# Mirrored Fourier columns, k transposed by transfers from pair 7 on, and pair 7's loads between the two weight matrices

## The chip, the cores and the metric

The kernel runs on one core of a Trainium2 chip. The metric is the device time of one execution in microseconds (us). The engines are named as in the profile: PE (TensorE, matrix products), DVE (VectorE), ACT (ScalarE), POOL (GpSimd), and SP (SyncE, which here only issues DMAs). PE writes to PSUM, which has eight banks of 512 f32 columns; POOL does not touch PSUM in this kernel.

## What is computed

A block-sparse attention (4 batches, 8 heads, 768 rows, 64 columns a head; each row sees its own block of 64 keys and up to three more that its gate scores pick, causally), and on its output a Fourier mix with a two-layer network:

```python
k_rep = k.reshape(B, H, n_blocks, block, D).mean(axis=3)
gate_scores = np.einsum('bhsd,bhnd->bhsn', q, k_rep)
gate_scores = np.where(causal, gate_scores, -1000000000.0)
top_idx = np.argsort(gate_scores, axis=-1)[..., -top_k:]
...
scores = np.where(mask & (pos[:, None] >= pos[None, :]), scale * q @ k.T, -1000000000.0)
x = softmax(scores) @ v
...
X = np.fft.fft(x, axis=1)
X = np.fft.fft(X, axis=2)
u = x + np.real(X)
un = (u - mu) / np.sqrt(var + 1e-06)
out = u + np.maximum(un @ w_ch1, 0.0) @ w_ch2
```

## The kernel before

All operations are first written down as a list (`Plan.op`: rank, engines with a cost in us, what is read and written). A planner (`Plan.schedule`, `Plan.search`) then places them on the engines by these costs, in simulated time, and after some hundred random changes of ranks and release times emits the program in the order found. So the order on each engine is fixed when the program is built, by the costs in the list; a change of a cost, of an operation or of the seed gives another order everywhere. `LANDING`, `LAT` and `SLACK` are what the planner adds for transfers, semaphores and PE's inputs; `rel` is the earliest time of an operation; `FILL_TO` says until when PE's waits are filled with matmuls on a tile of zeros (`warm`, `filler`, L476), which keep its clock up.

**Attention** (`attention(p)`) works on 16 pairs of heads, four pairs to a batch. A pair's q, k, v are loaded by SP (L453). POOL, ACT or DVE casts them to f16; q also gets the remainder of the cast, so that 128 rows (64 of the cast, 64 of the remainder) stand for a head in `qhl`. For pairs 0 to 6 PE transposes q (`q_turn`, L620) into PSUM, and DVE or ACT copies it to `QG`; from pair 7 on SP issues transposing transfers instead (L611). k's cast of all pairs is transposed by PE (`k_turn`, L564) and copied by ACT or DVE (L780, L781) to rows 0 to 63 of `KI`, whose rows 64 to 75 hold an indicator of the 12 key blocks. The block sums of k give the gate scores of q (L583, L600, L635, L640), DVE picks the best three of them (L674 and on), and the choice, turned by PE (L699), is written as 0 or -60000 into rows 64 to 75 of `QG` (L709). So the score product over 76 rows (L732) adds the mask by itself. ACT takes the exponential (L743), POOL cuts the diagonal blocks (L749), PE multiplies with v (L761), and DVE divides into `x` (L770, L773).

**Fourier** (`fourier(b)`) comes once all four pairs of a batch are there. It folds x by symmetry (L793, L804, L814), takes the first step over the rows on PE (`stage1`, L832, L836) with a copy to `ty` and a mirrored one to `tr`, and the second step over the columns for each of six row tiles (`stage2`, L866): two matmuls of 256 columns for the even and two for the odd output columns. DVE adds x (L872) and takes the statistics (L879, L882); the normed rows are transposed to `unT`, for batch 0's first half by PE (L930), otherwise by transfers of SP (L922).

**The network** (`mlp(b)`): `up` (L1034) with the ReLU on ACT or DVE (L1046, L1048), `down` (L1063) with the add to u (L1069) and the store. For the last batch `down` is done with seven products of quarter matrices instead of eight (`down_seven`, L1008, sums at L957 and L1014). The products of one batch lie between the attention of the next ones. POOL issues the loads of the two weight matrices (L457), with a cast on the way, w1 from 37 us and w2 from 51.4 us on in the planner's time.

`Plan.schedule` models POOL's and SP's transfers as sharing the bandwidth by half.

## Time and profile before

| | us |
|---|---|
| median of 3 runs | 295.85 (295.43 to 295.97) |
| the profiled execution | 295.36 |
| its span | 293.6 |
| PE busy | 287.7 |
| DVE busy | 210.5 |
| ACT busy | 185.0 |
| POOL busy | 129.2 |

The span runs from the first to the last instruction; 1.8 us lie around it. Busy time is the time in which an engine had at least one instruction in work; matmuls overlap one another, and fillers count as busy. In a group's row stand the line, engine, operation, out<-in, shapes and count, then the busy us and the mean ns of one, then the idle time just before them and what ended it.

### The profile page before, as it was taken

The numbers are of one execution on the slowest core, as the hardware profiler recorded it, in microseconds if no ns is written. First come the engines' busy times: TensorE is split into PE (matmuls) and PEld (weight loads), VectorE is DVE, ScalarE is ACT, GpSimd is POOL, SyncE is SP. The second block draws the span as 40 slices with busy tenths as digits, with TensorE's granted clock in tenths as the row PEclk, the third lists the DMA queues.
The fourth block names the chain that finished last, engine by engine and source line by source line (L and its number), as shares of the span: only waits on it lengthen the run. The fifth ranks groups of instructions, "written<-read, shape, count | busy, mean of one in ns | idle before, by whom it ended". The sixth has DMA issues, their size and how long they took to land.

```text
span 293.6 us, 8001 instructions
## 1 busy us (share of the span) xinstructions
PE 287.7 (98%) x3002; PEld 194.6 (66%) x3002; DVE 210.5 (72%) x704; ACT 185.0 (63%) x407; POOL 129.2 (44%) x251
## 2 busy tenths in 40 slices
PE   8999999999999999999999999999999999999995
PEld 4677777766656677567656776656766554566884
DVE  4899999995454869876458899589588801057884
ACT  3589998969718687478757747819941760577000
POOL 5568986765849618666731595823200000000000
PEclk9999999999999999999999999999999999999999
DMA  8999999999588951788596157470000403100132
GB/s 211 250 237 210 221 241 219 212 208 218 112 207 196 167 113 29 119 197 125 54 250 169 39 135 153 90 127 36 3 18 20 116 20 96 57 2 0 38 108 71
DMA packets 108773, 37.41 MB, mean 127 GB/s; under 512 B 101192, under 2 KB 104948, under 8 KB 108736
## 3 DMA queue, kind: packets, MB, share of 16 engines
q1 hardware_dynamic: 104272, 32.06, 50.4%
q0 software_dynamic: 3536, 4.56, 8.6%
q8 instruction: 23, 0.38, 0.6%
q10 hardware_dynamic: 928, 0.30, 0.4%
q14 instruction: 14, 0.11, 0.1%
HBM read 28.52 MB, written 6.29 MB: 119 GB/s over the span
## 4 chain that ended last, share of the span: by engine, by line
PE 89%; DVE 5%; ACT 2%; DMA 2%; issue 1%; POOL 0%; DVEq 0%; POOLq 0%
PE bank L1034 26%; PE bank L1063 21%; PE bank L732 12%; PE bank L761 7%; PE bank L1008 6%; PE bank L866 4%; PE bank L476 3%; DMA loads<-in_q_dram 2%; PE bank L564 1%; PE bank L620 1%; PE bank L832 1%; PE bank L583 1%; ACT ty L780 1%; PE bank L727 1%; DVE tr L781 1%
## 5 line engine op out<-in xcount | busy, mean ns | idle before, releaser
L743 ACT ACTIVATE turned<-bank 128x512 f16<-128x512 f32 (+1 forms) x192 | 89.7, 601 | 12.5 <-PE bank L732 12.1
L1034 PE MATMUL bank<-unT,w 128*128 128x384 f16 x512 | 90.7, 326 | 0.0
L1046 ACT ACTIVATE hT<-bank 128x384 f16<-128x384 f32 x114 | 56.7, 501 | 37.5 <-PE bank L1034 36.8
L1034 PEld LDWEIGHTS <-w 128*128 128x128 f16 x512 | 48.4, 98 | 29.7
L1063 PE MATMUL bank<-w,hT 128*128 128x512 f16 x288 | 67.9, 379 | 0.0
L732 PE MATMUL bank<-turned,keys 76*128 76x128 f16 (+3 forms) x384 | 51.2, 258 | 0.3 <-DVE tr L781 0.2
L1063 PEld LDWEIGHTS <-hT 128*128 128x128 f16 x288 | 26.6, 97 | 26.5
L749 POOL TENSOR_SCALAR_AFFINE_SELECT turned<-turned 128x512 f16<-128x512 f16 (+1 forms) x44 | 22.4, 529 | 38.8 <-ACT turned L743 28.0
L732 PEld LDWEIGHTS <-keys 76*128 76x128 f16 x384 | 29.8, 97 | 12.8 <-issue 0.5
L761 PEld LDWEIGHTS <-turned 128*128 128x128 f16 x672 | 23.7, 97 | 4.2 <-ACT turned L743 0.6
L1069 DVE TENSOR_TENSOR u<-bank,u 128x512 f32<-128x512 f32 x18 | 12.4, 689 | 19.3 <-PE bank L1063 19.1
L761 PE MATMUL bank<-vals,turned 128*128 128x65 f16 x672 | 25.1, 193 | 0.0
L552 POOL TENSOR_TENSOR loads<-loads 128x384 f16<-128x384 f32 x25 | 22.9, 915 | 4.1 <-DVE fs L793 3.1
L709 DVE TENSOR_SCALAR turned<-bank 12x384 f16<-12x384 f16 x64 | 20.6, 321 | 3.2 <-PE bank L699 1.4
L547 POOL TENSOR_TENSOR turned<-loads,turned 128x320 f16<-128x320 f32 x25 | 19.8, 792 | 1.4 <-DVE fs L793 0.8
L773 DVE TENSOR_TENSOR x<-bank,rcp 128x384 f16<-128x384 f32 x32 | 17.6, 553 | 0.8
L780 ACT COPY keys<-bank 64x768 f16<-64x768 f16 x14 | 11.1, 794 | 11.1 <-PE bank L564 8.6
L476 PE MATMUL bank<-warm 128*128 128x512 f16 x58 | 16.3, 412 | 1.3 <-DVE warm L464 1.3
L781 POOL CAST loads<-loads 128x384 f16<-128x384 f32 x24 | 12.3, 514 | 11.4 <-issue 3.0
L872 DVE TENSOR_TENSOR u<-bank,x 128x512 f32<-128x512 f32 x24 | 15.2, 670 | 0.9 <-PE bank L866 0.9
L879 DVE BATCH_NORM_STATS2 bst<-u 128x6 f32<-128x512 f32 x24 | 15.7, 671 | 0.0
L1014 DVE TENSOR_TENSOR u<-u,bank 128x256 f32<-128x256 f32 x36 | 13.1, 415 | 3.1 <-PE bank L1008 2.2
(110 smaller groups left out, 403.1 us busy)
## 6 DMA issues: line engine op xcount, KB each, us to landing
loads<-in_k_dram SPq DMA_DIRECT2D x28, 192.0 KB, 3.4
loads<-in_v_dram SPq DMA_DIRECT2D x28, 192.0 KB, 3.7
loads<-in_q_dram SPq DMA_DIRECT2D x26, 192.0 KB, 3.5
out_dram<-u SPq DMA_DIRECT2D x18, 256.0 KB, 2.3
w<-in_moe_w_ch_dram POOLq DMA_DIRECT2D x16, 256.0 KB, 6.9
out_dram<-u SPq DMA_DIRECT2D x12, 128.0 KB, 1.7
hT<-in_k_dram SPq DMA_DIRECT2D x4, 192.0 KB, 4.5
hT<-in_q_dram SPq DMA_DIRECT2D x4, 192.0 KB, 3.9
```

Of the source, the lines that this page charges most:

```text
L476: nc.tensor.matmul(bank32[P.SPARE], warm[:, 0:128], warm, start=True, stop=True)
L547: lambda x, n, hi=hi, lo=lo, e=e: eng[x].tensor_tensor(out=lo, in0=qn[a][:, e, 1:NST], in1=hi[:, 1:NST], op=OP.subtract),
L552: lambda x, n, kh=kh, kl=kl, e=e: eng[x].tensor_tensor(out=kl, in0=kn[a][:, :, e, :], in1=kh, op=OP.subtract),
L709: nc.vector.tensor_scalar(out=rows[:, i::2, :], in0=turned[at:at + NB, 0:3 - i, :], scalar1=-NEG, scalar2=NEG, op0=OP.mult, op1=OP.add)
L732: nc.tensor.matmul(bank32[sp.bank][:, co:co + a1 - a0], KI[e][g3][0:76, 128 * jt:128 * jt + 128], QG[e][g3][0:76, a0:a1], start=not added, ...
L743: lambda x, n, sp=sp, pt=pt, at=at, wid=wid: nc.scalar.activation(out=pt[:, at:at + wid], in_=bank32[sp.bank][:, 0:wid], func=AF.Exp, scal ...
L749: lambda x, n, pt=pt, at=at, nd=nd: nc.gpsimd.affine_select(out=pt[:, at:at + 128 * nd].rearrange("p (a c) -> p a c", a=nd), in_=pt[:, at: ...
L761: nc.tensor.matmul(o[:, st, 0:65], pt[:, col:col + 128], V16[v4][:, e, jt, 0:65], start=(i == 0), stop=(i == 20))
L1008: nc.tensor.matmul(bank32[mp.bank][:, 0:256], A[i][:, z, :], Bm[i][:, z, :], start=(z == 0), stop=(z == 7))
L1034: nc.tensor.matmul(bank32[hp_.bank][:, 0:384], w1[:, dt, 128 * it:128 * it + 128], unT[:, dt, 384 * hf:384 * hf + 384], start=(dt == 0), s ...
L1046: nc.scalar.activation(out=o, in_=i_, func=AF.Relu)
L1063: nc.tensor.matmul(bank32[cp.bank], hT[hf][:, it, 128 * j:128 * j + 128], w2[:, it, :], start=(it == 0), stop=(it == NIT - 1))
```

## The change

- Second Fourier step of batches 1 to 3 (`SYM`): the cosine part is even and the sine part odd in the column number, so the new `stage2_half` computes columns 0 to 255 of each part's half only (256, 129, 128 and 128 columns in four matmuls), laid out plainly in one bank. The mirrored columns come from it by sums: a copy of 256 columns out of PSUM (`bsb`), two adds of x of 256 columns out of PSUM, and two sums of 255 columns in SBUF on DVE or POOL. A 256-column table joins the constants.
- k of pairs 7 to 15 (`TURN_K`): k's cast goes into `kx`, 256 columns a row tile: indicator, k of head 0, k of head 1, indicator. SP's transposing transfers bring it to `KI` in two pieces a pair, and PE's transposes and the copies are left out. The two heads now have their rows in opposite order (`AT`), and head 0's scores run over 128 rows (`ROWS`) whose unused ones are zero in `KI`; `kx` and `KI` are prepared by memsets, and the indicator comes by four transfers instead of one.
- Loads: pair 7's wait for w1's last piece, w2 is issued from 55 us on, and loads may be released from 50 instead of 60 us.
- The planner shares bandwidth by `SHARE`, and searches 700 rounds with seed 8 (600 with seed 7 before).
- Memory: small tiles are cut from one, fewer buffers for `rcp` and `bst`, `lnv` joined with `nmr`, `warm` put on `bsb`. In `stage1` the extra matmuls on `xm` come earlier in the group.

```diff
...
@@ -89,6 +93,7 @@
     DEPTH = 5
+    SHARE = dict(POOL=1.5, SP=3.0)
@@ -290,7 +295,8 @@
                 shared = max(0.0, dma_free[other] - go)
-                dma_free[mine] = go + (2 * o.dma if 2 * o.dma <= shared else o.dma + shared / 2)
+                f = self.SHARE[mine]
+                dma_free[mine] = go + min(f * o.dma, o.dma + shared * (1.0 - 1.0 / f))
@@ -320,6 +326,9 @@
 LATE = 2600
+SYM = (1, 2, 3)
+W2 = 55.0
+TURN_K = 7
...
@@ -489,16 +510,30 @@
 
+    for i in range(NH):
+        small(3000, {"DVE": 0.5, "POOL": 0.9}, 0,
+              lambda x, n, i=i: [eng[x].memset(kx[i][:, :, at:at + 64], 0.0) for at in (0, 192)][-1],
+              w=[("kone", i)])
+
+        def ones(x, n, i=i):
+            flat = kx[i].rearrange("p s c -> p (s c)")
+            for lo in range(2):
+                for at in (lo, 192 + lo):
+                    r = eng[x].memset(flat[64 * lo:64 * lo + 64, at:at + 5 * 258 + 1:258], 1.0)
+            return r
+        small(3000, {"DVE": 0.24, "POOL": 0.62}, 0, ones, r=[("kone", i)], w=[("kone", i)])
+
...
 
-    def load(p, rank, what, e, q_="SP"):
+    def load(p, rank, what, e, q_="SP", r=()):
...
         dma(rank, q_, dst, src[b, 2 * hp + e].rearrange("(st p) d -> p st d", p=128),
-            [(t, i, e)], 0.72 if p < 3 else 0.85, rel=0.0 if p < 7 else max(60.0, release(p) - 18.0))
+            [(t, i, e)], 0.72 if p < 3 else 0.85, r=r,
+            rel=0.0 if p < 7 else max(50.0, release(p) - 18.0))
@@ -511,8 +546,12 @@
     const(0.6, "POOL", own24, dr["own24"].ap().rearrange("p (a c) -> p a c", a=5), ["own24"], 0.3, 3.3)
-    const(0.7, "POOL", ki_all[64:64 + NB], dr["IndR"].ap().unsqueeze(1)
-          .to_broadcast([NB, 2 * NG, S]), [("kind", e, i) for e in range(2) for i in range(NG)], 0.3, 4.0)
+    small(0.3, "DVE", 0.45, lambda x, n: nc.vector.memset(ki_all[0:64, :, :, 0, :], 0.0), w=["kz"])
+    for e in range(2):
+        for i in range(NG):
+            dma(0.7, "POOL", KI[e][i][64 - AT[e]:64 - AT[e] + NB],
+                dr["IndR"].ap().rearrange("n (s c) -> n s c", s=NST),
+                [("kind", e, i)], 0.1, r=["kz"] if e == 0 else [], rel=4.0)
@@ -530,13 +569,15 @@
             for e in range(2):
-                load(p, at_, "k", e)
-                load(p, at_, "q", e)
+                load(p, at_, "k", e, r=[("w1", 3, 1)] if p == HP + 3 else ())
+                load(p, at_, "q", e, r=[("w1", 3, 1)] if p == HP + 3 else ())
             for e in range(2):
-                load(p, at_ + (0.1 if p < 3 else 500), "v", e)
+                load(p, at_ + (0.1 if p < 3 else 500), "v", e,
+                     r=[("w1", 3, 1)] if p == HP + 3 else ())
         for e in range(2):
-            hi, lo = qhl[h2][:, e, :, 0:64], qhl[h2][:, e, 1:NST, 64:128]
-            kh, kl = k16[h2][:, :, 64 * e:64 * e + 64], klo[0][:, :, 64 * e:64 * e + 64]
+            hi = qhl[h2][:, e, :, AT[e]:AT[e] + 64]
+            lo = qhl[h2][:, e, 1:NST, 64 - AT[e]:128 - AT[e]]
+            kh, kl = kx[h2][:, :, 64 + 64 * e:128 + 64 * e], klo[0][:, :, 64 * e:64 * e + 64]
@@ -562,13 +603,23 @@
                 nc.tensor.transpose(bank16[tk.bank][:, 128 * st:128 * st + 128],
-                                    k16[h2][:, st, :], id16)
-        P.op(base + 10, {"PE": 0.34}, k_turn, r=["sm", ("k16", h2, 0), ("k16", h2, 1)],
-             w=[tk], ps=[tk], pre=[("ki", 0, g3), ("ki", 1, g3)])
+                                    kx[h2][:, st, 64:192], id16)
+        if p < TURN_K:
+            P.op(base + 10, {"PE": 0.34}, k_turn, r=["sm", ("k16", h2, 0), ("k16", h2, 1)],
+                 w=[tk], ps=[tk], pre=[("ki", 0, g3), ("ki", 1, g3)])
         for e in range(2):
+            if p >= TURN_K:
+                P.op(base + 16, {"SP": 1.4},
+                     lambda x, n, e=e: nc.sync.dma_start_transpose(
+                         out=ki_all[:, g3, 3 * e:3 * e + 3].rearrange("p s e c -> p (s e) c"),
+                         in_=kx[h2][:, 3 * e:3 * e + 3, :].rearrange("p s c -> p (s c)")),
+                     r=[("k16", h2, 0), ("k16", h2, 1), ("kone", h2)], w=[("ki", e, g3)],
+                     pre=[("ki", 1 - e, g3)], turn=True)
+                continue
             small(base + 11, {"DVE": 0.48, "ACT": 0.8}, 0,
-                  lambda x, n, e=e: _copy(x, KI[e][g3][0:64, :],
-                                          bank16[tk.bank][64 * e:64 * e + 64, 0:S]),
+                  lambda x, n, e=e: _copy(x, KI[e][g3][AT[e]:AT[e] + 64],
+                                          bank16[tk.bank][64 * e:64 * e + 64, 0:S]
+                                          .rearrange("p (s c) -> p s c", s=NST)),
...
@@ -730,13 +781,14 @@
                         nc.tensor.matmul(bank32[sp.bank][:, co:co + a1 - a0],
-                                         KI[e][g3][0:76, 128 * jt:128 * jt + 128],
-                                         QG[e][g3][0:76, a0:a1], start=not added,
+                                         KI[e][g3][0:ROWS[e], jt, :],
+                                         QG[e][g3][0:ROWS[e], a0:a1], start=not added,
...
                      r=[("ki", e, g3), ("kind", e, g3), ("qg", e, g3), ("qm", e, g3)]
+                     + ([("ki", 1 - e, g3)] if p >= TURN_K else [])
...
@@ -865,27 +917,69 @@
                                          start=(j == 0), stop=(j == 1))
-            P.op(base + late + 4, {"PE": 0.44}, stage2, r=[("ty", i) for i in range(4)] + [("trv", i) for i in range(4)]
-                 + ["cds"],
-                 w=[mp], ps=[mp], pre=[("u", u2, kt)])
-            small(base + late + 4, "DVE", 0.61,
-                  lambda x, n, kt=kt, mp=mp: nc.vector.tensor_tensor(
-                      out=U[:, kt, :].rearrange("p (l r) -> p r l", r=2),
-                      in0=bank32[mp.bank].rearrange("p (r l) -> p r l", r=2),
-                      in1=X[:, kt, :].rearrange("p (l r) -> p r l", r=2), op=OP.add),
-                  r=[mp] + xall, w=[("u", u2, kt)], ps=[mp])
+            def stage2_half(x, n, kt=kt, mp=mp):
+                half = tyf if kt < 3 else trf
+                o, at = bank32[mp.bank], 128 * (kt % 3)
+                lhs = lambda i: half[i][:, at:at + 128]
+                nc.tensor.matmul(o[:, 0:256], lhs(2), cdsf[:, 3 * DM:3 * DM + 256],
+                                 start=True, stop=False)
+                nc.tensor.matmul(o[:, 0:129], lhs(0), cds[:, 0, 0:129], start=False, stop=True)
+                nc.tensor.matmul(o[:, 256:384], lhs(1), cds[:, 0, 256:384], start=True, stop=True)
+                nc.tensor.matmul(o[:, 384:512], lhs(3), cds[:, 2, 256:384], start=True, stop=True)
+
+            if b in SYM:
+                P.op(base + late + 4, {"PE": 0.29}, stage2_half,
+                     r=[("ty", i) for i in range(4)] + [("trv", i) for i in range(4)] + ["cds"],
+                     w=[mp], ps=[mp])
+                ub_, uk, i2 = U[:, kt, :], ("u", u2, kt), kt % 2
+                uh = [("uh", u2, kt, i) for i in range(2)]
+                x_ = X[:, kt, :]
+                duo = lambda t: t.rearrange("p (m r) -> p r m", r=2)
+                rows = lambda n_, mp=mp: bank32[mp.bank][:, 0:n_].rearrange("p (r m) -> p r m", r=2)
+                small(base + late + 4, {"ACT": 0.38, "DVE": 0.33}, 0,
+                      lambda x, n, i2=i2, rows=rows: _copy(x, duo(bsb[i2]), rows(512)[:, :, 128:256]),
+                      r=[mp], w=[("bsb", i2)], ps=[mp])
+                small(base + late + 4, "DVE", 0.34,
+                      lambda x, n, ub_=ub_, x_=x_, rows=rows: nc.vector.tensor_tensor(
+                          out=duo(ub_[:, 0:256]), in0=rows(512)[:, :, 0:128],
+                          in1=duo(x_[:, 0:256]), op=OP.add),
+                      r=[mp] + xall, w=[uh[0]], ps=[mp], pre=[uk])
+                small(base + late + 4, "DVE", 0.34,
+                      lambda x, n, ub_=ub_, x_=x_, rows=rows: nc.vector.tensor_tensor(
+                          out=duo(ub_[:, 256:512]), in0=rows(510)[:, :, 128:0:-1],
+                          in1=duo(x_[:, 256:512]), op=OP.add),
+                      r=[mp] + xall, w=[uh[1]], ps=[mp], pre=[uk])
+                signs = (OP.subtract, OP.add) if kt < 3 else (OP.add, OP.subtract)
+                small(base + late + 4, {"DVE": 0.32, "POOL": 0.62}, 0,
+                      lambda x, n, ub_=ub_, i2=i2, op=signs[0]: eng[x].tensor_tensor(
+                          out=ub_[:, 1:256], in0=ub_[:, 1:256], in1=bsb[i2][:, 1:256], op=op),
+                      r=[uh[0], ("bsb", i2)], w=[uh[0]], port=True)
+                small(base + late + 4, {"DVE": 0.32, "POOL": 0.62}, 0,
+                      lambda x, n, ub_=ub_, i2=i2, op=signs[1]: eng[x].tensor_tensor(
+                          out=ub_[:, 257:512], in0=ub_[:, 257:512], in1=bsb[i2][:, 255:0:-1], op=op),
+                      r=uh + [("bsb", i2)], w=[uh[1], uk], port=True)
...
@@ -1089,7 +1183,7 @@
             for g in range(8):
-                weight(51.4 + 1.8 * g, w2[:, 2 * g:2 * g + 2, :],
+                weight(W2 + 1.8 * g, w2[:, 2 * g:2 * g + 2, :],
@@ -1100,7 +1194,7 @@
     with tc.manual_schedule():
-        for o in P.search(600, 7):
+        for o in P.search(700, 8):
```

More of the change, by code (lines that the diff above doesn't have):

```diff
@@ L388 @@
     ltri = sm[:, 392:520]
[L389 to L399 removed]
+    eps, ind32 = spare(2, FP), spare(4, FP)
+    cz24, own24 = (spare(120, BF).rearrange("p (a c) -> p a c", a=5) for _ in range(2))
+    vals_ = spare(2376)
     def cut(t, at, n, *dims, dtype=F16):
@@ L479 @@
     for i in range(NH):
-        small(0, "DVE", 0.07, lambda x, n, i=i: nc.vector.memset(qhl[i][:, :, 0, 64:128], 0.0),
-              w=[("qz", i)])
+        small(0, "DVE", 0.07, lambda x, n, i=i: [nc.vector.memset(qhl[i][:, e, 0, 64 - AT[e]:128 - AT[e]], 0.0)
+                                    for e in range(2)][-1], w=[("qz", i)])
     for i in range(2):
@@ new lines, in fourier @@
+            if b in SYM:
[29 more added lines that the diff above has]
+                      r=uh + [("bsb", i2)], w=[uh[1], uk], port=True)
+            else:
+                P.op(base + late + 4, {"PE": 0.44}, stage2, r=[("ty", i) for i in range(4)] + [("trv", i) for i in range(4)]
+                     + ["cds"],
+                     w=[mp], ps=[mp], pre=[("u", u2, kt)])
+                small(base + late + 4, "DVE", 0.61,
+                      lambda x, n, kt=kt, mp=mp: nc.vector.tensor_tensor(
+                          out=U[:, kt, :].rearrange("p (l r) -> p r l", r=2),
+                          in0=bank32[mp.bank].rearrange("p (r l) -> p r l", r=2),
+                          in1=X[:, kt, :].rearrange("p (l r) -> p r l", r=2), op=OP.add),
+                      r=[mp] + xall, w=[("u", u2, kt)], ps=[mp])
@@ L884, in fourier @@
+                  r=[("bst", kt % 2)], w=[("st", u2, kt)])
         for hf in range(2):
```

96 lines of the change are left out of this document (52 added, 44 removed).

## The prediction, made before the changed kernel ran

> **What bounds the kernel now.** I read the top of the page, then the busy time by stretches of the span, then what TensorE (PE) waited for, then the chain of waits, and the groups of instructions last. The page:
>
> ```profile
> span 293.6 us, 8001 instructions
> PE 287.7 (98%) x3002; PEld 194.6 (66%) x3002; DVE 210.5 (72%) x704; ACT 185.0 (63%) x407; POOL 129.2 (44%) x251
> ```
>
> By stretches (columns: stretch, its length, then busy us of PE, PE's weight loads, DVE, ACT and POOL with counts, clock, DMA share, GB/s); the last row is the same view of the filler matmuls of L476 alone:
>
> ```profile
> 40.00:60.00 20.00, 19.75 (x284) 15.60 (x281) 18.92 (x57) 18.20 (x44) 15.06 (x26) 1.00 1.14 225
> 60.00:75.00 15.00, 15.00 (x157) 9.92 (x154) 10.53 (x39) 12.44 (x27) 9.45 (x20) 1.00 1.21 201
> 75.00:90.00 15.00, 15.00 (x144) 8.66 (x141) 8.61 (x31) 4.99 (x11) 10.15 (x20) 1.00 0.70 163
> 90.00:110.00 20.00, 19.47 (x220) 13.98 (x219) 13.22 (x43) 16.14 (x38) 10.35 (x22) 1.00 0.77 162
> 210.00:230.00 20.00, 20.00 (x175) 12.90 (x172) 16.85 (x37) 7.88 (x20) 0.41 (x1) 1.00 0.08 27
> 60.00:75.00 15.00, 2.27 (x9) 0.76 (x9) 1.00 1.21 201
> ```
>
> Until about 60 us DVE and ACT are 91 to 95% busy, the DMA is full, and PE's waits are stuffed with filler matmuls: this front part is not PE's. From 60 us on PE is full while DVE and ACT have room. All that PE waited for between 60 and 292 us is this (engine, line, releaser, us in total, times, longest):
>
> ```profile
> PE bank L866 <- DVE tr L781: 0.3, 1, 0.3
> PE bank L732 <- DVE tr L781: 0.2, 1, 0.2
> ```
>
> A busy PE need not be a full one, since a matmul's shown duration contains its drain. So I take PE's price from the chain of waits, where pieces in succession are not counted twice (start, us, what):
>
> ```profile
> 115.46 0.33 PE bank L564 x6
> 169.19 2.62 PE bank L866 x24
> 225.17 5.18 PE bank L1063 x24
> 230.35 10.40 PE bank L1034 x64
> 240.75 10.36 PE bank L1063 x48
> 251.11 20.80 PE bank L1034 x128
> 271.91 18.35 PE bank L1008 x168
> ```
>
> The last five pieces follow one another without a gap for 65 us, at 162.5 ns per matmul of 384 columns and 109 ns per matmul of 256: that is 2.4 columns per ns and about 2.5 ns more for each matmul. So columns are what is paid, and the weight load that each of them has is covered even under a 109 ns matmul. From 60 us to the end every column taken away should come off the end, as long as nothing else runs out.
>
> **The change part by part.** *Fourier columns.* For batches 1, 2 and 3 the second Fourier step, L866, takes four matmuls of 256, 129, 128 and 128 columns for a row tile instead of four of 256. Now a tile costs 2.62/6 = 0.437 us. A 128-column matmul with its own weight load costs 0.33/6 = 0.056 us (L564 above), so a new tile costs 0.109 + 3 x 0.056 = 0.277 us. Saved: 0.160 us a tile, 18 tiles, 2.9 us, all on the path. Batch 0, whose step falls into the front where DVE is full, keeps the old form.
>
> *k of pairs 7 to 15.* Nine times six transposing matmuls of L564 go: 9 x 0.33 = 3.0 us, also on the path. That the score matmuls of one head now contract 128 rows instead of 76 costs nothing: their columns, which are what PE pays, stay the same. Together PE loses **5.9 us** of work behind 75 us.
>
> *What DVE, ACT and POOL pay.* The rows (line, engine, operation, shapes, count, busy, mean ns, idle before; the two keys rows give minimum, median and maximum instead and are those after 70 us):
>
> ```profile
> L872 DVE TENSOR_TENSOR u<-bank,x 128x512 f32<-128x512 f32 x24 | 15.2, 670 | 0.9 <-PE bank L866 0.9
> L1014 DVE TENSOR_TENSOR u<-u,bank 128x256 f32<-128x256 f32 x36 | 13.1, 415 | 3.1 <-PE bank L1008 2.2
> L552 DVE TENSOR_TENSOR loads<-loads 128x384 f16<-128x384 f32 x1 | 0.6, 558 | 0.0
> L552 POOL TENSOR_TENSOR loads<-loads 128x384 f16<-128x384 f32 x25 | 22.9, 915 | 4.1 <-DVE fs L793 3.1
> L780 ACT CAST ty<-bank 128x386 f16<-128x386 f32 x16 | 8.9, 605 | 5.2 <-PE bank L832 2.3 <-PE bank L836 1.6 <-DVE tr L781 1.3
> L780 ACT COPY keys<-bank x9: 782/796/797, 76.4 to 190.3; 64x768 f16<-64x768 f16 x9
> L781 DVE COPY keys<-bank x9: 540/549/560, 77.2 to 189.7; 64x768 f16<-64x768 f16 x9
> ```
>
> The one add of 670 ns becomes two of 256 columns, 415 ns each by L1014: +0.16 us a tile, 2.9 us in all on DVE. A copy of 256 columns out of PSUM is new; no row shows it, its bounds are 0.4 us (256/386 of L780's 605 ns) and that row's whole 0.6, and I take 0.45: 18 x 0.45 = 8.1 us, on ACT if the planner chooses so. Two sums of 255 f32 columns inside SBUF are new too; on DVE they lie between 255/384 of L552's 558 ns, 0.37 us, and the whole 0.56, and I take L1014's 0.42, its size being the nearest; on POOL between 0.61 and 0.92 by its L552 row, and I take 0.67. All 36 on DVE are 15.1 us, all on POOL 24 us. Against this the copies of k to KI go: 9 x 0.80 = 7.2 us of ACT and 9 x 0.55 = 4.9 us of DVE. So ACT is about even and DVE gains at worst 2.9 + 15.1 - 4.9 = 13 us, spread from 75 to 230 us. What hides it is PE work of the other batches. For the last batch the cover is the longest row of pieces above: the second Fourier step ends at 225.17 and its first product, the piece of 128, starts at 251.11, 26 us later. DVE's extra for the first three tiles is 3 x (0.16 + 0.84) = 3 us, for all six 6 us; the cover holds these. If it were gone the price would be up to 3 us a batch, 9 us.
>
> *Transposing transfers for k.* Eighteen more on SP's queue, next to 18 for q. The rows are the issue on SP (minimum, median, maximum ns), the landing, a stretch in which two transposes and nothing else start, a crowded stretch, the wait of SP's queue, the issue for pair 15's q, and the mask written for that pair, which its scores need:
>
> ```profile
> L611 SPq DMA_TRANSPOSE turned<-turned x18: 1210/1241/2110, 75.0 to 192.1; - x18
> DMA to landing us min/median/max: 2.5/2.6/5.2
> 144.00:145.00 1.00, 1.00 (x8) 0.61 (x7) 0.42 (x2) 0.96 (x2) 1.00 (x2) 1.00 2.79 145
> 95.00:100.00 5.00, 5.00 (x72) 3.63 (x71) 3.39 (x19) 3.16 (x7) 3.98 (x9) 1.00 1.13 187
> SPq L611 <- POOL loads L552: 26.0, 9, 8.8
> 190.79 2.58 SPq L611 DMA_TRANSPOSE turned<-turned  x2
> 203.32 1.38 DVE L709 TENSOR_SCALAR turned<-bank 12x384 f16<-12x384 f16 x4
> ```
>
> SP is busy 18 x 1.24 = 22 us more over the 117 us of that first row. Behind a transpose that waits for POOL's cast stand the loads of later pairs, the output stores and the transposes of unT; the loads run pairs ahead. For pair 15 q's transposes are issued by 193.37, and the mask, which comes out of q by way of the gates, is done at 204.70. If k's two go behind q's, they add 2 x 1.24 us of issue and 2.6 us of landing and are there at 198.5, 6.2 us before the scores can start. So the path at 0 us. The DMA engines pay 2.79/2 = 1.4 us for each, 25 us over the same 117; in the crowded stretch, where the share is above 1 already, they and their neighbours land later. Their bounds: 0, or as in the second rival below.
>
> *Loads and the start.* Pair 7's loads now wait for w1's last piece, and w2 is issued 3.6 us later; four index transfers, a zeroing of KI and the memsets of kx come into the start:
>
> ```profile
> L457 POOL DMA_DIRECT2D w<-in_moe_w_ch_dram x16: 544/640/736, 37.2 to 66.5; - x16
> 78.44 0.86 PE bank L1063 x4
> 2.10 0.38 DVE L489 MEMSET xm<- 128x384 uint32 x1
> 2.58 0.16 DVE L471 MEMSET ind<- 64x1 f32 x2
> 4.43 0.36 DVE L781 CAST turned<-loads 128x384 f16<-128x384 f32 x1 [1.69 <-DMA loads<-in_q_dram]
> 4.52 0.60 POOL L505 DMA_DIRECT2D keys<-c_IndR  x1
> 8.55 0.50 POOL L781 CAST loads<-loads 128x384 f16<-128x384 f32 x1 [2.89 <-DVE ka L593]
> ```
>
> POOL idles 2.89 us before 8.55, and three more issues are 1.8 us: hidden. DVE idles 1.69 us before 4.43. The zeroing has 768 words a row, 0.76 us at twice the xm row, and kx's memsets are about 0.7 us for each of two buffers (384 words like xm, and four small ones of 0.08): 2.2 us against 1.69. Some of that may go to POOL; bounds 0 and 2 us, and I take 0.3. w2's last issue moves from 66.5 to about 70 and was needed from 78.44 on, so it lands just in time or PE takes other work first. Pair 7 matters for the hole in ACT from 75 to 90 (4.99 of 15 us busy): coming earlier it can only help, and at best it replaces the 2.27 us of fillers between 60 and 75 by work. I take 0; bounds -2.3 and +2 us.
>
> *Sum.* The profiled execution took 295.36 us, 293.6 of it the span. 295.36 - 2.9 - 3.0 + 0.3 = 289.8. That execution lies 0.49 us below the median of the runs, 295.85, so for a median I say **290.2 us**. About 0.2% (0.6 us) is what a measurement of this kernel can tell from no change.
>
> **The rivals.** *PE is only busy, not full.* Then the saved work becomes idle time and the kernel stays at 295.4 to 295.9. For it speaks that weight loads cover only 66% of the span; against it the five gapless pieces. [...] Chance 0.05.
>
> *k lands too late (slower).* Place: pairs 8 to 10, around 90 to 110 us, where the DMA share is 1.13 and PE's only two waits lie. Four transposes more are 5.6 us of DMA there; with a landing of 5.2 instead of 2.6 us and SP held as now for up to 8.8 us behind POOL, k comes 2 to 5 us after the mask instead of 6.2 before. Three pairs at 3.5 us are 10.5 us: 290.2 + 10.5 = **300.7 us**. It decides from 6 us of delay on; slower than before needs more than 5.7 us of stall in all. For it: SP's 26 us of waiting at these very transposes. Against it: k needs only POOL's first casts, q also the subtractions after them, so k may even go first. Chance 0.09.
>
> *The longer way to unT shows.* DVE's 3 us before the first half of each batch, with POOL and DVE in each other's way, comes out uncovered in batch 1 (90 to 110 us, where PE stood still already) and partly in batch 2: 3 to 4.5 us of the gain are lost, 293.2 to 294.7 us. [...] Chance 0.13; that all three batches lose 3 us and more, which ends at 299 or above, 0.03.
>
> *More than the PE work.* Pair 7's earlier arrival removes the fillers and the 0.5 us of waits: 290.2 - 2.8 = 287.4. Chance 0.12.
>
> **How the numbers follow.** The sum as it stands, 288.5 to 292, has 0.58. Faster by over 0.2%: 0.58 + 0.13 + 0.12 = 0.83. Same: 0.05. Slower: 0.09 + 0.03 = 0.12. The range goes from 286.8 (the fillers' gain and a little of the order's own luck) to 295.0 (the gain lost but for the last us); it leaves out the slower cases and half of no change. The likeliest case alone is 288.5 to 292.
>
> **What would show it.** Right: L866's group splits and a tile of batches 1 to 3 takes 0.28 us in the chain; L564 has 42 matmuls instead of 96; SP shows 36 such transposes instead of 18; PE has no wait above 0.5 us after 60 us; DVE shows 36 adds of about 415 ns. Wrong: waits of PE's score matmuls (L732's successor) for a DMA of keys between 80 and 110 us; fillers growing before 75 us; PE idle before the up products of batches 1 to 3; or PE idle by what was saved.

## The result, and the profile after

The changed kernel takes **297.82 us** (median of 10 runs, 296.17 to 299.84) against 295.78 us before (10 runs, 295.43 to 295.97): a ratio of 1.0068, interval 1.0045 to 1.0092. It is slower by 2 us where 290.2 us was predicted; the range began at 286.8 and ended at 295.0. The profiled execution took 297.6 us. The page of the changed kernel:

```profile
span 295.9 us, 7996 instructions
PE 286.0 (97%) x2959; PEld 191.4 (65%) x2959; DVE 217.7 (74%) x755; ACT 183.4 (62%) x413; POOL 137.6 (47%) x266
```

By stretches, as before (stretch, length, busy us of PE, PE's weight loads, DVE, ACT, POOL, then granted clock, DMA share, GB/s):

```profile
60.00:75.00 15.00, 14.89 (x154) 9.35 (x152) 13.32 (x51) 11.43 (x27) 9.40 (x19) 1.00 1.04 163
75.00:90.00 15.00, 15.00 (x145) 8.99 (x144) 7.79 (x29) 7.30 (x18) 9.36 (x21) 1.00 1.01 197
90.00:110.00 20.00, 20.00 (x208) 13.81 (x207) 13.95 (x42) 13.79 (x33) 10.32 (x22) 1.00 0.96 189
150.00:155.00 5.00, 3.08 (x30) 1.71 (x29) 1.13 (x4) 1.08 (x3) 1.24 (x3) 0.93 1.09 157
210.00:230.00 20.00, 20.00 (x155) 11.38 (x154) 14.10 (x40) 10.30 (x24) 2.44 (x8) 1.00 0.09 31
```

All that PE waited for between 60 us and the end:

```profile
PE bank L783 <- DMA keys<-loads: 1.9, 1, 1.9
PE bank L1128 <- DVE u L948: 0.3, 1, 0.3
```

The short waits of 90 to 110 us are gone and a long one has come at 152 us: scores (now L783) that wait for a transposing transfer of k. The rest of the loss is at the start, which is seen in when the first product of the feed-forward part, `up`, begins (first and last start at the end of the row). Before:

```profile
L1034 PE MATMUL bank<-unT,w x512: 322/326/328, 63.8 to 271.6; 128*128 128x384 f16 x171
```

After:

```profile
L1128 PE MATMUL bank<-unT,w x512: 322/326/337, 67.8 to 273.7; 128*128 128x384 f16 x171
```

So the span splits into two parts that can be judged apart: up to the first `up`, 63.8 us before and 67.8 after (+4.0), and from there to the end, 229.8 us before and 228.1 after (-1.7; from the rows as rounded, so good to 0.1). The prediction had +0.3 and -5.9.

The parts of the change themselves cost what was forecast. A tile of the second Fourier step in the chain of the changed kernel:

```profile
235.33 0.11 PE bank L924
235.44 0.06 PE bank L926
235.50 0.06 PE bank L927
235.55 0.06 PE bank L928
```

That is 0.28 us a tile against 0.277 forecast. The groups of DVE, ACT and POOL (by shape; count, busy us, mean ns):

```profile
L948 DVE TENSOR_TENSOR u<-bank,x 128x256 f32<-128x256 f32 x18 | 7.5, 415 | 0.0
L943 DVE TENSOR_TENSOR u<-bank,x 128x256 f32<-128x256 f32 x18 | 7.4, 410 | 0.1
L832 ACT COPY bsb<-bank 128x256 f32<-128x256 f32 x15 | 6.1, 407 | 4.9 <-DVE u L958 4.1 <-POOL u L958 0.7
L954 DVE TENSOR_TENSOR u<-u,bsb 128x255 f32<-128x255 f32 x10 | 4.0, 411 | 0.0
L958 POOL TENSOR_TENSOR u<-u,bsb 128x255 f32<-128x255 f32 x5 | 3.6, 723 | 3.9 <-issue 2.4 <-DVE u L954 1.5
```

Forecast were 0.42 us for an add, 0.45 for the copy, 0.42 (DVE) and 0.67 (POOL) for a sum. What all of this costs PE is the 0.3 us of waiting for `u` above.

### The profile page after: what moved, and what is told of

Read it like the earlier page. It is cut to its first block, busy times and chain, and to the rows that moved or that the text cites. A ratio compares the mean times of both kernels' runs of the same rounds, so it can differ in the third digit from the quotient of the medians.

```text
span 295.9 us, 7996 instructions
## 1 busy us (share of the span) xinstructions
PE 286.0 (97%) x2959; PEld 191.4 (65%) x2959; DVE 217.7 (74%) x755; ACT 183.4 (62%) x413; POOL 137.6 (47%) x266
## 4 chain that ended last, share of the span: by engine, by line
PE 80%; DVE 8%; SPq 4%; DMA 3%; ACT 3%; issue 1%; POOL 0%; ACTq 0%
PE bank L1128 27%; PE bank L1157 20%; PE bank L783 11%; PE bank L1102 6%; PE bank L813 6%; SPq L475 3%; PE bank L884 2%; DMA loads<-in_v_dram 2%; DMA keys<-loads 2%; PE bank L497 1%; ACT turned L795 1%; PE bank L634 1%; PE bank L750 1%; PE bank L778 1%; DVE turned L760 1%
## 5 line engine op out<-in xcount | busy, mean ns | idle before, releaser
L795 ACT ACTIVATE turned<-bank 128x512 f16<-128x512 f32 x192 | 90.6, 585 | 32.0 <-PE bank L783 21.5
L783 PE MATMUL bank<-turned,keys 128*128 128x128 f16 (+7 forms) x384 | 51.7, 261 | 2.0 <-DMA keys<-loads 1.9
L783 PEld LDWEIGHTS <-keys 76*128 76x128 f16 (+1 forms) x384 | 30.1, 98 | 15.2 <-DMA keys<-loads 2.1
L813 PE MATMUL bank<-small,turned 128*128 128x65 f16 x672 | 25.2, 193 | 0.0
L497 PE MATMUL bank<-bsb 128*128 128x512 f16 x69 | 18.7, 402 | 1.3 <-DVE bsb L486 1.3
L825 DVE TENSOR_TENSOR x<-bank,small 128x384 f16<-128x384 f32 x32 | 17.7, 553 | 0.7
L973 DVE BATCH_NORM_STATS2 small<-u 128x6 f32<-128x512 f32 x24 | 16.0, 678 | 0.1
L954 POOL TENSOR_TENSOR u<-u,bsb 128x255 f32<-128x255 f32 x8 | 5.8, 725 | 20.8 <-DVE u L958 16.1
L833 POOL CAST small<-loads 128x384 f16<-128x384 f32 x23 | 11.3, 505 | 7.9 <-PE bank L928 3.0
L833 POOL CAST turned<-loads 128x384 f16<-128x384 f32 x25 | 12.7, 507 | 4.0 <-DMA loads<-in_q_dram 1.8
```

Of the source, the lines that this page charges most:

```text
L497: nc.tensor.matmul(bank32[P.SPARE], warm[:, 0:128], warm, start=True, stop=True)
L783: nc.tensor.matmul(bank32[sp.bank][:, co:co + a1 - a0], KI[e][g3][0:ROWS[e], jt, :], QG[e][g3][0:ROWS[e], a0:a1], start=not added, stop=no ...
L795: lambda x, n, sp=sp, pt=pt, at=at, wid=wid: nc.scalar.activation(out=pt[:, at:at + wid], in_=bank32[sp.bank][:, 0:wid], func=AF.Exp, scal ...
L813: nc.tensor.matmul(o[:, st, 0:65], pt[:, col:col + 128], V16[v4][:, e, jt, 0:65], start=(i == 0), stop=(i == 20))
L833: return eng[x].tensor_copy(out=dst, in_=src)
```

## Experiments: the late piece of k

The chain of the changed kernel from 143 to 154 us (start, us, what; SPq is SP issuing):

```profile
143.26 1.28 SPq L613
...
144.59 0.58 SPq L475
...
147.96 0.93 SPq L475
...
148.93 4.62 DMA keys<-loads
...
153.59 0.96 PE bank L783 x6
```

Pair 11's first piece of k is issued at 143.26; then SP issues the six loads of pair 13, 4.3 us, and only at 148.93 the second piece, which lands behind those loads, 4.62 us later. PE stands still from 151.7 to 153.6. What comes next costs as much again (the same columns as above, microsecond by microsecond):

```profile
152.00:153.00 1.00, 0.00 (x0) 0.00 (x0) 0.00 (x0) 0.00 (x0) 0.00 (x0) 1.00 0.41 82
154.00:155.00 1.00, 1.00 (x17) 0.58 (x15) 0.11 (x1) 1.00 (x3) 0.41 (x1) 0.64 0.78 155
155.00:156.00 1.00, 1.00 (x5) 0.45 (x4) 0.23 (x2) 1.00 (x4) 0.59 (x2) 0.50 0.62 121
156.00:157.00 1.00, 1.00 (x5) 0.45 (x4) 0.00 (x0) 0.48 (x1) 0.00 (x0) 0.50 0.88 195
157.00:158.00 1.00, 1.00 (x13) 0.85 (x11) 0.03 (x1) 0.70 (x2) 0.00 (x0) 0.66 1.03 273
```

The granted clock falls to half, for 3.4 us. PE looks fully busy, but 0.36 + 0.50 + 0.50 + 0.34 = 1.7 us of its work are missing.

My theory: these 3.6 us are one instruction in the wrong place on SP. In all experiments on the changed kernel but two, which say so, the planner's order was frozen, so that only the edit differs.

**a1_second_piece.**

```diff
 SP's order:  k piece 0 of pair 11
+             k piece 1 of pair 11
              k, q, v loads of pair 13 (six)
-             k piece 1 of pair 11
```

> The changed kernel in its own order, with one instruction moved: the second of pair 11's two transposing transfers of k is issued on SP right behind the first, not behind the six loads of pair 13. Theory late piece: TensorE's wait of 2.1 us before pair 11's scores (151 to 154 us) goes, and with it the stretch right behind it in which the granted clock fell to 0.55, some 1.7 us: 297.8 - 3.8 = 294.0 us. Rival 1, the clock falls for another reason (the load of the chip at that place): only the wait goes, 295.7 us. Rival 2, something else is late right behind (the gates, pair 13's loads): within 1 us of 297.8 us.

Measured: 295.18 us (293.86 to 295.84), ratio 0.9968 to before (0.9951 to 0.9984). The wait and the half clock are gone:

```profile
150.00:155.00 5.00, 5.00 (x49) 3.00 (x47) 1.59 (x6) 3.16 (x8) 1.86 (x4) 1.00 0.95 182
155.00:160.00 5.00, 5.00 (x71) 3.24 (x70) 2.92 (x16) 2.39 (x7) 2.49 (x9) 1.00 0.83 185
```

The profiled span is 292.3 us, 3.6 less than the 295.9 of the changed kernel; from the first `up` on it is 292.31 - 67.86 = 224.5 us instead of 228.1. The median moved by 2.6 us, less. Part of the reason may be that the clock does not fall in every execution of the changed kernel: its run at a mean clock of 1.000 took 296.17 us, those at 0.994 took 297.3 to 298.5. But a1's ten runs also hold three at 0.993 (295.3 to 295.5 us, among 293.9 to 295.8), and no trace shows where the clock fell in them; the profiled execution of a1 is one of its fastest, so 3.6 us is the difference of two executions and not of the medians.

## Experiments: the start

In the changed kernel everything of the first 17 us comes later, and the DMA is why: from 5 to 12 us, a 256-byte packet of the loads has a median duration of 25 ns in its trace, and 18 ns in the trace of before. In GB/s (last column), before:

```profile
4.00:8.00 4.00, 4.00 (x34) 2.85 (x32) 2.39 (x7) 1.19 (x3) 1.59 (x3) 1.00 1.22 309
8.00:12.00 4.00, 3.71 (x65) 2.68 (x63) 3.66 (x12) 2.83 (x5) 2.61 (x4) 1.00 1.26 262
```

After:

```profile
4.00:8.00 4.00, 3.18 (x25) 2.08 (x23) 1.55 (x9) 1.09 (x3) 3.10 (x6) 1.00 1.26 234
8.00:12.00 4.00, 3.12 (x54) 2.36 (x52) 2.99 (x8) 1.72 (x4) 0.79 (x1) 1.00 1.32 208
```

The DMA engines are as busy as before and move a quarter less. Three candidates: the new memsets, the four index transfers, and where the loads are written, because the change also lays out SBUF anew.

**a2_late_pads.**

```diff
-memsets of kx's pads: in the first 4 us
+memsets of kx's pads: ahead of the first op planned behind 60 us
```

> The changed kernel in its own order, with the four memset groups of the pads of kx moved from the first 4 us to about 60 us, ahead of the first transposing transfer that reads them. Theory pads at the start: they hold up POOL's first transfers by 0.7 us and DVE by about as much, and everything behind shifts with them; without them the first scores come 1 to 2 us earlier than at 20.6 us, up starts 1 to 2 us earlier than at 68.0 us, and the time falls by as much, to 296 to 297 us. Rival, the loads are slow for another reason: first scores and up where they were, 297.8 us give or take 0.6.

Measured: 300.58 us (298.18 to 301.52), first `up` at 70.4. The packets stay at 25 ns and the first score product starts at 18.7 us instead of 17.4, not earlier. The theory of the pads falls, and the other way round: at 60 us the memsets are on the path, in its chain,

```profile
65.13 0.64 POOL turned L812
65.77 0.73 POOL loads L518 x2
66.86 0.42 DVE loads L518 x2
```

where at the start they were hidden.

**a3_no_index.**

```diff
-four transfers of IndR into KI
+nc.gpsimd.memset(ki_all[64:76, :, :, 1, :], 0.0)
```

> The changed kernel in its own order, without the four transfers of the block index rows into KI; a single memset on POOL fills the rows, so that the mask of the gates is left out of the computation. Theory index transfers: their 1536-byte packets run beside the loads from 7 to 10 us and are why the 256-byte packets take 25 ns instead of 18; without them the packets take 18 ns from about 7 us on, the first scores come near 16 us and up starts near 64 us: 297.8 - 4 = 294 us. Rival, the packets are slow from 4.3 us on, before the first of these transfers, so for another reason: 25 ns as before, time within 1 us of 297.8 us.

Measured: 297.84 us (297.06 to 299.28), 25 ns, first `up` at 67.5: 0.4 us earlier, no more. The index transfers are not the cause.

**a4_shift.** The tiles ahead of that of the loads take 38400 bytes in the changed kernel (`cds` 3584, two `bsb` of 1024, `w1` and `w2` of 16384), so it starts at 0 modulo 256. In the kernel before they take 42112 (by the tile list, each rounded up to 32 bytes): 128 modulo 256. Here and in the runs that follow, such remainders are counted from the first tile of the kernel's list. The address in SBUF is 128 more modulo 256, since four constants lie ahead of the list; what that means is told in the last section.

```diff
+    mx8 = many(2, [128, 5, 2, 8], FP, "mx8")    # 640 bytes
     loads_ = sb([128, 13056], F16, "loads")
...
-    mx8 = many(2, [128, 5, 2, 8], FP, "mx8")
```

> The changed kernel in its own order, with a small tile (mx8) allocated ahead of the tile of the loads, so that the loads and all tiles between start 640 bytes later, at 128 modulo 512 as in the kernel before instead of 0 modulo 512. Theory placement: the 256-byte packets are slow because of where they are written; they go back to a median of 18 ns from 4 to 17 us, first scores near 16 us, up near 64 us, 294 us. Rival: nothing of that moves, 297.8 us give or take 0.6.

Measured: 294.36 us (293.83 to 294.97), ratio 0.9951 (0.9932 to 0.9970). Packets take 18 ns again, in

```profile
4.00:8.00 4.00, 4.00 (x33) 2.81 (x31) 2.47 (x11) 1.71 (x4) 3.16 (x6) 1.00 1.22 309
```

and `up` begins at 65.3:

```profile
L1139 PE MATMUL bank<-unT,w x512: 322/326/336, 65.3 to 270.6; 128*128 128x384 f16 x171
```

That such a move of a tile does it was a guess among three, so the next runs try to break it.

**b2_before_at_0** makes the kernel before slow in the same way:

```diff
+    mx8 = many(2, [128, 5, 2, 8], FP, "mx8")             # 640 bytes
+    tr0 = sb([128, KM - 1, 2], F16, "tr_0")              # 768 bytes
     loads_ = sb([128, 11520], F16, "loads")              # was 128, now 0 modulo 512
```

> The kernel before, with mx8 and tr_0 allocated ahead of the tile of the loads, so that it starts at 0 modulo 512 as in the changed kernel, instead of at 128. Nothing else changes. Theory placement of the loads: packets of 256 bytes take 25 ns from 4 us on, k1, q and v land 1 to 3 us later, up starts 2 to 4 us later than at 63.95 us, 298 to 299.5 us. Rival, the placement matters only together with the changed kernel's other tiles or transfers: 295.85 us and 18 ns as before.

Measured: 298.57 us (298.14 to 299.25), ratio 1.0098 (1.0081 to 1.0114).

```profile
4.00:8.00 4.00, 3.81 (x27) 2.33 (x24) 1.39 (x4) 0.51 (x1) 1.58 (x3) 1.00 1.27 233
```

`up` begins at 67.0 instead of 63.8, and from there on it takes 229.8 us, as before. So the placement alone costs the old kernel 2.9 us, all of it at the start.

**b4_behind** and **b3_shift256** ask which tile it is and which multiple:

```diff
     loads_ = sb([128, 13056], F16, "loads")
+    mx8 = ...                        # b4: behind the loads, moves only what follows
```
```diff
+    tr0 = sb([128, KM - 1, 2], F16, "tr_0")   # b3: 768 bytes, loads at 256 modulo 512
     loads_ = sb([128, 13056], F16, "loads")
```

> The changed kernel in its own order, with mx8 between the tile of the loads and that of the turned rows: the loads stay at 0 modulo 512, and the tiles behind them (turned, keys, small ones) move by 640 bytes. Theory placement of the loads: nothing changes, 25 ns and 297.8 us. Rival, it is the tiles behind (casts, constants, index rows) whose placement matters: 18 ns and 294.4 us.

> The changed kernel in its own order, with tr_0 (768 bytes) ahead of the tile of the loads, which then starts at 256 modulo 512. Theory whole packets: what is slow is a 256-byte packet written at a multiple of 256, so 256 is as slow as 0: packets of 25 ns, 297.8 us. Rival whole 512: only 0 modulo 512 is slow, 18 ns, 294.4 us. Rival chance (any move of the tiles shuffles it): in between.

Measured: b4 297.75 us (296.90 to 297.88), b3 298.54 us (297.84 to 299.55), both at 25 ns. It is the tile of the loads, and 256 is as bad as 0.

**b1_both** puts a1 and a4 together.

> The changed kernel in its own order with both edits that helped: pair 11's second piece of k right behind its first, and mx8 ahead of the tile of the loads. Theory two separate losses: they add, 297.8 - 2.6 - 3.4 = 291.8 us (290.5 to 292.5), with no wait of TensorE over 0.5 us behind 60 us; that is within 1.6 us of the predicted 290.2 us, so the saved columns of TensorE did come off the end. Rival, one loss seen twice (a later start only moves the late piece, or the other way round): 294 us again.

Measured: **291.66 us** (291.51 to 291.75), ratio 0.9862 (0.9847 to 0.9876): the two losses add, and the change is faster than the kernel before by 4.1 us. Its page and its only wait behind 60 us:

```profile
span 290.0 us, 7996 instructions
PE 284.4 (98%) x2959; PEld 190.8 (66%) x2959; DVE 217.5 (75%) x755; ACT 183.3 (63%) x413; POOL 137.5 (47%) x266
```
```profile
PE bank L1139 <- DVE u L959: 0.3, 1, 0.3
```

**c3_shift64, d1_shift384, d2_shift192** try three more places in b1, with one `mx8` (64 modulo 256), both `mx8` and `tr_0` (128 modulo 256, but 384 modulo 512), and the two `kg` (192 modulo 256) ahead of the loads.

> The version with both edits (291.66 us), in the same order, where only one of the two mx8 tiles (320 bytes) lies ahead of the tile of the loads, which so starts at 64 modulo 256 instead of 128. Theory multiples of 256 are slow and nothing else is: packets of 18 ns, 291.7 us. Rival, only 128 is fast (halves of 256): 25 ns, 295.2 us. In between if a packet's cost goes by how far it is off.

> The version with both edits (291.66 us), in the same order, with tr_0 (768 bytes) also ahead of the tile of the loads, which then starts at 384 modulo 512, that is 128 modulo 256. Theory the remainder by 256 decides: 18 ns, 291.7 us. Rival, only 128 modulo 512 is fast: 25 ns, 295.2 us.

> The version with both edits (291.66 us), in the same order, with the two kg tiles (192 bytes) instead of the mx8 tiles ahead of the tile of the loads, which then starts at 192 modulo 256. Theory only 128 modulo 256 is fast: 25 ns from 5 us on, 295.2 us. Rival, 64 was slow for a reason of its own and 192 is fast: 291.7 us.

Measured: c3 295.07 us (294.06 to 298.28), d1 292.08 us (291.95 to 292.42), d2 295.31 us (294.34 to 296.22). From 4 to 8 us c3, d1 and d2 show:

```profile
4.00:8.00 4.00, 3.85 (x26) 2.32 (x24) 1.62 (x9) 1.13 (x3) 3.05 (x6) 1.00 1.27 231
```
```profile
4.00:8.00 4.00, 4.00 (x20) 2.30 (x18) 2.41 (x11) 1.53 (x3) 3.00 (x6) 1.00 1.20 307
```
```profile
4.00:8.00 4.00, 3.43 (x27) 2.26 (x24) 1.59 (x9) 1.12 (x3) 3.08 (x6) 1.00 1.27 230
```

Counted from the first tile, 0, 64 and 192 modulo 256 are slow (230 to 236 GB/s from 4 to 8 us) and 128 is fast (307 to 314). By address in SBUF that is 128, 192 and 64 slow, and of these four places only the multiple of 256 fast. The remainder by 512 made no difference in either pair that differs in it: d1 moves 307 GB/s and b1 308, b3 233 and the changed kernel 234.

**e1_hT_too** carries the rule to `hT` (96 counted from the first tile, 224 modulo 256 by address), whose second half takes the loads of pairs 2 and 5.

```diff
-    gsb = many(2, [128, 5, 24], FP, "gsb")
+    gsb = [None, sb([128, 5, 24], FP, "gsb_1")]
     hT = many(2, [128, NIT, 384], F16, "hT")             # 96 -> 128 modulo 256
+    gsb[0] = sb([128, 5, 24], FP, "gsb_0")
```

> The version with both edits (291.66 us), in the same order, with one of the two gsb tiles allocated behind hT instead of ahead of it, so that hT, whose second half takes the loads of pairs 2 and 5, starts at 128 modulo 256 instead of 96; the tile of the loads stays at 128. Theory the rule holds for every tile that takes such packets: the packets into hT at 10 to 14 and 28 to 31 us, of which a tenth still took 27 to 28 ns, all take 18 ns, and what waits for pairs 2 and 5 comes earlier by up to 0.5 us: 291.2 to 291.6 us. Rival 1, their slowness has another source: nothing moves, 291.7 us. Rival 2, they land in the shadow of DVE's work: 18 ns, but 291.7 us.

Measured: 291.98 us (291.55 to 292.39). Rival 2: at 10 to 14 us and at 28 to 31, when `hT` is loaded, nine packets in ten now take at most 18 ns, against 22 and 24 ns in b1, and the time does not move. Those pairs land in the shadow of other work.

## Experiments: is PE full, and the rest

**c1_turns_again** and **c2_columns_again** put the removed work back into b1 without any use for it:

```diff
+            if p >= TURN_K:                     # c1, in k_sums, over-written by the sums
+                for st in range(NST):
+                    nc.tensor.transpose(bank16[ks.bank][:, 128 * st:128 * st + 128],
+                                        kx[h2][:, st, 64:192], id16)
```
```diff
+                nc.tensor.matmul(o[:, 0:384], lhs(2), cds[:, 0, 0:384], start=True, stop=True)   # c2
                 nc.tensor.matmul(o[:, 0:256], lhs(2), cdsf[:, 3 * DM:3 * DM + 256],
```

> The version with both edits (291.66 us), in the same order, where TensorE does the six transposing matmuls of k for pairs 7 to 15 once more, ahead of the sums of k, into the same PSUM bank, while the transposing transfers stay: 54 matmuls more, which nobody reads. Theory columns are paid: 9 x 0.33 = 3.0 us more, 294.6 us. Rival, TensorE is only busy and not full: less than 1 us more, under 292.7 us.

> The version with both edits (291.66 us), in the same order, where each of the 18 tiles of the second Fourier step of batches 1 to 3 gets one more matmul of 384 columns, which is written over: the 1024 columns of the old form, in a different cut. Theory columns are paid: 18 x 0.16 = 2.9 us more, 294.5 us. Rival, TensorE is only busy and not full: less than 1 us more, under 292.7 us.

Measured: c1 293.81 us (293.75 to 294.00), +2.15; c2 293.80 us (293.53 to 294.20), +2.14. From the first `up` to the end the profiled executions take 226.9 and 227.2 us against 224.5: +2.4 of 3.0 and +2.7 of 2.9. So columns are paid behind 65 us, at 80 to 93% of the forecast price by these two executions and at 72 to 74% by the medians; c1 has no wait left where b1 has 0.3 us for `u`. What the columns are worth is 4.3 us of the 5.9, by the medians, if the two add up; no run has both.

**c4_old_seven** and **d3_other_order** are planned anew, both with the loads at 128 modulo 256 and with no load between two pieces of k. c4 takes back what the change does to pair 7 and to w2; d3 keeps it and searches as the kernel before did.

```diff
-W2 = 55.0                                          # c4
+W2 = 51.4
-    r=[("w1", 3, 1)] if p == HP + 3 else ()        # c4, three times
+    r=()
-    max(50.0, release(p) - 18.0)                   # c4
+    max(60.0, release(p) - 18.0)
```
```diff
-        for o in P.search(700, 8):                 # d3
+        for o in P.search(600, 7):
```

> The version with both edits, planned anew with pair 7's loads and w2 as in the kernel before: no wait of pair 7 for w1's last piece, its release at 60 us, w2 from 51.4 us on. Theory pair 7 is worth nothing either way, as the prediction had it: 291.7 us give or take 0.8, which a new order alone can move. Rival 1, pair 7 between the weights fills the hole of ACT at 75 to 90 us: up to 2.3 us slower without it, 294 us. Rival 2, it is what still makes up start 1.7 us later than in the kernel before (65.5 against 63.8 us): up near 64 us, 290 us.

> The changed kernel with the loads at 128 modulo 256, planned by the search of the kernel before (600 steps, seed 7 instead of 700 and 8), and no load between a pair's two pieces of k. Theory the gain is the columns' and not one order's: 291.7 us give or take 1.5. Rival, the order found with 700 steps is a lucky one: 294 us or more, like the version with pair 7 as before (295.43 us), whose loss would then be the order's as well.

Measured: c4 295.43 us (294.98 to 295.87), d3 293.86 us (293.50 to 294.21). Another order alone is worth 2.2 us, so the 3.8 us of c4 are not pair 7's for certain: its own part, 1.6 us if d3 is the fair comparison, stays open. Shown is that the gain survives another order (d3's ratio to before is 0.9933, 0.9918 to 0.9948) and that orders differ by more than I allowed for. The traces also show where they differ. The first `up` begins at 68.8 us in c4 and 68.4 in d3, with 80 and 75 fillers ahead of it, and from there on they take 224.6 and 223.2 us, no more than b1's 224.5. So in all three orders the part behind the first `up`, where the columns were saved, is 5.2 to 6.6 us shorter than the 229.8 of before, and the losses lie ahead of it. A later `up` may leave less work behind itself, so this does not price the columns in c4 and d3. `up` near 64 us, c4's rival 2, did not come.

## Why the prediction was wrong, step by step

Sum by parts, from the profiled executions (us; spans and first `up`):

| part | forecast | measured | b1 |
|---|---|---|---|
| up to the first `up` | +0.3 | +4.0 (63.8 to 67.8) | +1.7 (65.5) |
| from there, without the late piece (forecast: columns) | -5.9 | -5.3 (229.8 to 224.5, in a1) | -5.3 (224.5) |
| k of pair 11 | 0 | +3.6 (224.5 to 228.1) | 0 |
| sum | -5.6 | +2.3 (293.6 to 295.9) | -3.6 |

- *Fourier columns and k's transposes on PE*: right in mechanism and nearly in size (-5.3 of -5.9 behind the first `up`, of which putting the columns back shows 4.3 by the medians). 0.28 us a tile, 42 transposing matmuls left, 36 adds at 410 to 415 ns. The rival that PE is only busy is refuted by c1 and c2. The weight loads' share, which spoke for it, is 66% in b1 too, where 54 useless matmuls still cost 2.15 us. Nor is a matmul's shown duration its price: in the trace of the changed kernel the score products over 128 rows show medians of 219, 272, 326 and 379 ns for 128, 256, 384 and 512 columns, by these four some 165 ns beyond what grows with the columns, while `up` pays 162.5 ns for 384 (128 in 20.80 us of the chain, as before). Over 76 rows the medians are 218, 271.5, 327 and 379 ns, so the longer contraction of one head cost nothing that is seen.
- *DVE's extra work hidden by PE*: right; 0.3 us of waiting for `u`. That POOL and DVE would be in each other's way there was my supposition and did not show in the durations: a sum took 411 to 431 ns on DVE and 723 to 725 on POOL (means of the two lines), where 0.42 and 0.67 us were forecast.
- *Transposing transfers for k, "so the path at 0 us"*: wrong, and here the step is plain. I looked at what stands behind a transpose on SP (loads, stores) and at pair 15, where nothing else is queued. I didn't look at what the planner can put ahead of the second of two pieces. A row of before that hinted at it was quoted: a landing of up to 5.2 us. The rival "k lands too late" had the mechanism but another place (pairs 8 to 10 instead of 11), three pairs instead of one, and no clock: one wait of 1.9 us cost 3.6.
- *Loads and the start, +0.3 with bounds 0 and 2*: the term that failed most, +4.0. Its operations were costed rightly (memsets hidden, index transfers 0.4 us); the cause was not in the list of operations at all. The new layout of SBUF moved the tile of the loads from 128 to 0 modulo 256, that is from an address that is a multiple of 256 to one that is not: 2.3 to 2.6 us (a4, b1), 3.2 us in the kernel before (b2). The remaining 1.7 us arise behind the start: the first score product begins at 15.1 us in b1, at 15.0 before. They go with the new order: fillers are up from 58 to 69 matmuls, and by d3 an order can move the time that much. Which of its choices, is not shown.

```profile
L497 PE MATMUL bank<-bsb 128*128 128x512 f16 x69 | 18.7, 402 | 1.3 <-DVE bsb L486 1.3
```

- *Pair 7, 0*: not settled (c4 and d3).

With the two accidents mended the kernel takes 291.66 us, 1.5 above the forecast and inside its range. Part of that is the order's luck, since d3, with the same two mended, takes 293.86 us. The forecast was one for the arithmetic of the change, and the loss is in what came along with it.

## What to carry to other kernels

Read a diff for what it moves in memory, too: a reordered list of tiles is a change of every transfer's destination, and here it cost 2.9 to 3.4 us, more than either of the two intended savings brought (2.15 each). Work such a place out as an address in SBUF, to which everything ahead of the kernel's own list adds too (here 128 modulo 256). Where an operation is split into two transfers on one queue, ask what the scheduler may put between them, and issue them back to back. Split a missed sum at a landmark that both traces have (here the first `up`): it showed that the forecast saving had come and that two other things had eaten it.

## What the runs showed of the hardware

**Where 256-byte packets are written.** In the nine kernels whose tile of the loads starts at 0, 64 or 192 modulo 256, counted from the first tile of the list (after, a1, a2, a3, b2, b3, b4, c3, d2) the packets take a median of 25 ns from 5 to 12 us, and the DMA moves 230 to 236 GB/s from 4 to 8 us; in the nine at 128 (before, a4, b1, c1, c2, c4, d1, d3, e1) it is 18 ns and 307 to 314 GB/s. There is no exception. Ahead of the list, though, every one of these programs as built allocates 16384 bytes for the DMA and four constants at 16384, 16416, 16448 and 16480, 32 bytes each, which POOL sets first; in the changed kernel:

```profile
0.31 0.10 POOL L1217 MEMSET const-float32-0.0<- 128x1 f32 x1 [0.31 <-issue]
0.34 0.11 POOL L1217 MEMSET const-float32-1.0<- 128x1 f32 x1
0.38 0.11 POOL L1217 MEMSET const-bfloat16-1.0<- 128x1 bf16 x1
0.41 0.11 POOL L1217 MEMSET const-uint8-127<- 128x1 uint8 x1
```

So an address in SBUF is the count plus 128 modulo 256. The nine fast kernels are exactly those that write the packets to multiples of 256 (the tile of the loads is at 58624 before and 55552 in b1); the slow ones are 128 off (54912 after), or 192 (c3), or 64 (d2). What sets the two apart is the place of the writes: 18 ns a packet at a multiple of 256, 25 ns at the other three places. What costs the 7 ns there is not shown: only places were tried, no mechanism.

**The clock after a short idle.** In the changed kernel 1.9 us without a matmul brought the granted clock to 0.50 for 3.4 us: two whole microseconds of the view above, and parts of two more, which show 0.64 and 0.66. The traces of a2, a3, b3 and b4, which wait at the same place for 1.7 to 2.4 us, show 0.50 for 3.41 us as well. In a4 a wait of 1.8 us did not bring it down:

```profile
150.00:152.00 2.00, 0.24 (x4) 0.06 (x2) 0.00 (x0) 0.00 (x0) 0.00 (x0) 1.00 1.00 151
152.00:154.00 2.00, 1.97 (x24) 1.30 (x25) 0.34 (x2) 1.64 (x4) 0.97 (x2) 1.00 0.50 112
```

In all these traces a stretch at full clock lasts a whole number of 3.413 us (in the changed kernel 150.19 us, 44 of them, ahead of the fall, and 139.95, 41 of them, behind it; in the kernel before 290.13, 85 of them), and the stretch at 0.50 is one of them. The fall so comes at the end of such a step, there at 154.3 us, when PE was back at work. The step before the fall was not idle throughout: PE was busy for 1.49 us of it in the changed kernel and for 1.97 in a3; in a4's, which held the wait too, it was 1.65 and the clock stayed. Busy time alone does not tell which way it goes. From PE's first matmul to 60 us, where the fillers stand in its waits, it stood still for 0.88 us at most in the changed kernel and for 0.28 before, and the clock is at 1.00 in both. In the changed kernel 1.9 us of waiting cost 3.6 in all; by that one case a wait of that length is to be priced at up to twice itself.
